# Linear attention and a highway layer: whole-row query packets, head-half exponentials, tanh + 1 on GpSimd

## The chip, the cores and the metric

The kernel runs on one core of one Trainium2 chip. The metric is the device time of one execution in microseconds; several runs are taken and the median counts.

## The reference

```
q_s = exp(q - max_d q);  q_s = q_s / (sum_d q_s + 1e-9)
k_s = exp(k - max_s k);  k_s = k_s / (sum_s k_s + 1e-9)
kv  = einsum('bhsd,bhse->bhde', k_s, v)
a   = einsum('bhsd,bhde->bhse', q_s, kv)          # 8 batches, 8 heads, 576 rows, 64 columns
x   = a.transpose(0, 2, 1, 3).reshape(4608, 512)
H   = maximum(x @ w_h, 0)
T   = 1 / (1 + exp(-(x @ w_t + b_t)))
out = T * H + (1 - T) * x                         # 4608 x 512, float32
```

q, k, v, the two 512 x 512 weights and the bias come as float32.

## The kernel before

**Tiles.** The 576 rows of a batch are 64 groups (partitions) of 9 neighbouring rows j = 0 to 8. A landing tile of k, q or v holds a batch as 128 partitions (two heads of a pair, 64 groups each) by 4 head pairs by 9 x 64 columns. The output is made in 36 tiles of 128 rows by 512 columns: four tiles for each batch (jp = 0 to 3, two values of j each) and one tile that two batches share, for the ninth row of each group. Nine tiles belong to a pair of batches: tiles 0 to 3 to batch 0, 4 to 7 to batch 1, tile 8 to both, and so on.

**Steps.** Everything is written as short steps whose order is the string `ORDER` (lines 15 to 61): a step is `name_tile_part` or `name_batch_part`, with a letter behind a colon where the engine is a choice (A is ScalarE, D is VectorE, P is GpSimd, called POOL in the profile). Each engine takes its instructions in that order, and so does SP, which issues nearly all transfers. Waits between engines follow from the data and from the reuse of buffers.

For a batch: `k`, `q`, `v` load (SP). `ek` takes the exponential of k (ScalarE, L252), `vc` casts v to 16 bits (L258, on any of three engines). `kv` is 72 small matmuls over j (L268). `kr` and `kn` take the reciprocal of the sums and scale into a block-diagonal tile `kvb` (VectorE, L280, L286). `eq` takes the exponential of q (ScalarE, L297, L303, L305), `qt` turns it with 18 transposes (TensorE, L316, L321) in three groups: j 0 to 3, j 4 to 7, j 8. `qc` copies the turned block out of PSUM (L330).

For a tile: `xu` multiplies turned q by `kvb` (L350), and the sums come as further columns. `rs` and `x` divide on VectorE (L359, L365). `xt` turns x (L372) and `xe` copies it out (L379). `bw` puts the bias into the bank `tps` (a ScalarE copy L387, or a matmul L389), `mt` adds x @ w_t to it (L399), `mh` makes x @ (w_h - 1)/2 in `gps` (L407). `th` is tanh of half the gate (ScalarE, L421, L423), `dd` is d = max(-x/2, gps) (VectorE, L427). The output is x + (tanh + 1) d. For 19 tiles `uu` does (tanh + 1) d in one VectorE instruction from PSUM (L442) and `oo` adds x on POOL (L460). For the 17 others, called lifted, which `ORDER` marks with `uu_i_0:P`, ScalarE writes tanh to SBUF and POOL does three two-input operations: `ee` e = d + x (L433), `uu` u = tanh d (L440), `oo` u + e (L460). `st` stores (L468, L476, L480).

**Buffers.** Landing tiles of each of k, q, v: 3. Tiles of x: 6. d, tanh, u, e: 3 each. Turned q: 4. Banks in PSUM: `tps` 2, `gps` 2, one area for `xu` and `kv`, one bank for `qt`, one for `xt`.

**Packets.** For batches 0 to 3 a query row is one run of 9 x 64 floats, 2304 bytes (batches 0 and 1 in two cuts). For batches 4 to 7 (`WIDE`) the query comes in a layout of its own: the main part in runs of four rows (1024 bytes), in two transfers, each on every second partition, and the row j = 4 of each group, 256 bytes, in a third transfer with an own place in `ORDER` (`q_4_9` to `q_7_9`). In the WIDE layout two output tiles that are mates are stored in one transfer of 128 partitions; for batches 0 to 3 in two transfers of 64 partitions each (`st_1_0`, `st_1_1`), in both cases in runs of 4096 bytes.

The copy of the turned queries, before:

```
t = eqp.tile([P, a, 4, s * NP], FP16, ...)
copy(t.rearrange("p a n t -> p (a n t)"), T[f"qps{b}_{g}"].rearrange("p a n s t -> p (a n s t)"))
```

Of the kernel before, what the change touches and what calls it, by code (L numbers as in the profile page):

```python
# [20 lines left out]
xe_1_0:D k_1_0 bw_1 xu_3_0 q_1_4 wtc_0 xu_0_1 rs_3_0 x_3_0 mh_1_0 wtc_2 xt_3_0 xe_3_0 xu_2_0 mt_1_0 rs_0_1 x_0_1 xt_0_0  # L21
eq_1_0 q_2_0 mt_3_0 th_1_0 rs_2_0 xe_0_0:D vc_1_3 ek_1_3 x_2_0 xt_0_1 th_3_0 qt_1_0 xe_0_1:D ek_1_2 dd_1 vc_1_0:A mh_0_0
xt_2_0 k_2_0 xe_2_0:D vc_1_2:D uu_1_0:P mh_0_1 bw_2 dd_0 qc_1_0:A mh_2_0 ee_1 dd_2 vc_1_1 v_2_0 kv_1_1 mh_3_0 ek_1_0
bw_0 kr_1_1 kn_1_1 dd_3 ek_1_1 mt_2_0 xu_5_1 rs_5_1 xu_4_1 kv_1_0 rs_4_1 k_3_0 x_5_1 th_2_0 kr_1_0 bw_5 oo_1_0 xt_5_1
mt_0_1 kn_1_0 mt_0_0 xu_5_0 x_4_1 rs_5_0 eq_1_1 ee_2 xu_4_0 qt_1_1 xe_5_1 mt_5_1 x_5_0 eq_1_2 qc_1_1 xt_5_0 xe_5_0:D
mh_5_1 th_0_0 q_3_0 rs_4_0 eq_2_2 uu_0_0 xu_6_0 rs_6_0 xt_4_1 qt_1_2 mt_5_0 mh_5_0 v_3_0 bw_4 x_4_0 x_6_0 xe_4_1 th_5_0
xt_4_0 mh_4_1 uu_3_0:P qc_1_2:A xe_4_0 xu_8_0 mh_4_0 mt_4_1 xt_6_0 ee_3 mt_4_0 eq_2_0 dd_5 oo_0_0 uu_2_0:P rs_8_0 oo_3_0
vc_2_2 uu_5_0 qt_2_0 x_8_0 ek_2_2 xe_6_0:D ek_2_0 k_4_0 dd_4 xu_7_0 rs_7_0 bw_6 th_4_0 oo_5_0 xt_8_0 mh_6_0 mt_6_0 q_4_9
x_7_0 xe_8_0:D xt_7_0 vc_2_0:A qc_2_0 eq_2_1 uu_4_0 oo_4_0 dd_6 bw_7:A kv_2_0 th_6_0 bw_8:A ek_3_0 ek_3_2 oo_2_0
xe_7_0:D mh_8_0 kr_2_0 kn_2_0 dd_8 mt_7_0 xu_9_0 rs_9_0 x_9_0 qt_2_1 th_7_0 mt_8_0 ee_6 q_4_0 qc_2_1 uu_6_0:P xu_10_0  # L30
oo_6_0 xt_9_0 rs_10_0 x_10_0 th_8_0 xe_9_0 mh_7_0 uu_8_0 qt_2_2 dd_7 bw_9 xu_12_0 eq_3_1 eq_3_0 xt_10_0 mt_9_0 mh_9_0
rs_12_0 x_12_0 xe_10_0:D uu_7_0:P xu_11_0 qc_2_2 xt_12_0 rs_11_0 qt_3_0 x_11_0 bw_10:A vc_3_2 dd_9 xe_12_0:D vc_3_0:A
th_9_0 uu_9_0 mh_10_0 oo_8_0 kv_3_0 kr_3_0 dd_10 ee_7 xt_11_0 mt_10_0 eq_3_2 qc_3_0:A bw_12:A oo_7_0 kn_3_0 mh_12_0
xu_14_0 ek_4_2 mt_12_0 xe_11_0:D v_4_0 v_5_0 qt_3_1 ek_4_0 rs_14_0 x_14_0 dd_12 xt_14_0 xe_14_0:D k_5_0 xu_13_0 th_10_0
bw_11:A rs_13_0 mh_11_0 mt_11_0 x_13_0 th_12_0 q_5_0 xt_13_0 qc_3_1:A oo_9_0 ee_10 dd_11 uu_10_0:P xu_15_0 qt_3_2
uu_12_0 rs_15_0 mh_14_0 eq_4_0 xe_13_0:D eq_4_1 mh_13_0 x_15_0 oo_10_0 xu_16_0 xt_15_0 qc_3_2 dd_14 rs_16_0 qt_4_0 ee_11
th_11_0 bw_14:A k_6_0 mt_14_0 x_16_0 qc_4_0 vc_4_2:A xe_15_0:D st_1_1 xu_17_0 st_1_0 rs_17_0 oo_12_0 x_17_0 qt_4_1 dd_13
bw_13:A mt_13_0 th_14_0 fill_0 vc_4_0 kv_4_0 uu_11_0:P eq_4_2 xt_16_0 qc_4_1:A mh_15_0 v_6_0 qt_4_2 vc_5_2 q_5_9 uu_14_0
xe_16_0:D st_3_1 oo_11_0 kr_4_0 th_13_0 oo_14_0 kn_4_0 bw_16:A bw_15:A xt_17_0 ek_5_0 xe_17_0:D dd_15 mh_16_0 xu_18_0
qc_4_2:A rs_18_0 mt_16_0 ek_5_2 x_18_0 vc_5_0 th_16_0 uu_13_0:P mt_15_0 dd_16 uu_16_0 xt_18_0 kv_5_0 kr_5_0 ee_13 ee_15  # L40
eq_5_0 xe_18_0:D kn_5_0 mh_17_0 mh_18_0 dd_17 xu_20_0 th_15_0 eq_5_1 bw_17:A rs_20_0 st_5_1 st_3_0 bw_18:A ek_6_0 qt_5_1
x_20_0 qc_5_1 mt_17_0 xu_21_0 rs_21_0 oo_13_0 xt_20_0 uu_15_0:P x_21_0 mt_18_0 ek_6_2 qt_5_0 xe_20_0:D oo_16_0 st_5_0
xu_19_0 xt_21_0 mh_20_0 oo_15_0 th_17_0 ee_17 dd_18 q_6_0 q_7_0 rs_19_0 th_18_0 st_7_1 uu_18_0 bw_20:A vc_6_0 qc_5_0:A
mt_20_0 x_19_0 xu_22_0 uu_17_0:P xe_21_0:D dd_20 rs_22_0 st_7_0 bw_21:A xt_19_0 mh_21_0 th_20_0 x_22_0 vc_6_2:A mt_21_0
kv_6_0 k_7_0 xe_19_0 st_10_0 uu_20_0 mh_19_0 th_21_0 oo_17_0 kr_6_0 xt_22_0 kn_6_0 dd_21 bw_19:A mt_19_0 xe_22_0:D
xu_23_0 v_7_0 bw_22 rs_23_0 mt_22_0 th_19_0 x_23_0 eq_5_2 bw_23:A qt_5_2 oo_18_0 xu_24_0 dd_19 xt_23_0 rs_24_0 mh_22_0
xe_23_0:D x_24_0 mh_23_0 eq_6_0 eq_6_1 qc_5_2 xt_24_0 xu_25_0 oo_20_0 dd_22 ee_21 rs_25_0 x_25_0 qt_6_0 xe_24_0:D
th_22_0 mt_23_0 uu_21_0:P ee_19 xu_26_0 qc_6_0 xt_25_0 st_10_1 bw_24:A st_12_1 oo_21_0 rs_26_0 eq_7_1 x_26_0 dd_23
eq_7_0 th_23_0 uu_22_0:P xe_25_0:D mh_24_0 fill_0 qt_7_0 mt_24_0 uu_19_0:P ee_22 xu_27_0 uu_23_0 rs_27_0 qc_7_0:A
oo_19_0 dd_24 xt_26_0 bw_25:A qt_6_1 oo_22_0 mh_25_0 xe_26_0 q_7_9 qc_6_1 x_27_0 mt_25_0 th_24_0 ek_7_2 xu_29_0 rs_29_0  # L50
mh_26_0 x_29_0 bw_27:A xt_27_0 uu_24_0:P qt_7_1 xe_27_0:D q_6_9 dd_25 xu_28_0 rs_28_0 xt_29_0 th_25_0 mt_27_0 mh_27_0
uu_25_0 oo_23_0 ek_7_0 vc_7_0 vc_7_2:A x_28_0 bw_26:A ee_24 kv_7_0 xe_29_0:D st_12_0:A dd_26 xt_28_0 th_27_0 kr_7_0
mt_26_0 kn_7_0 dd_27 bw_29:A eq_6_2 oo_25_0 oo_24_0 th_26_0 xe_28_0:D eq_7_2 mh_29_0 qc_7_1:A xu_31_0 mt_29_0 uu_26_0
ee_27 st_14_0 th_29_0 bw_28:A rs_31_0 x_31_0 mh_28_0 st_21_0 dd_29 xu_30_0 rs_30_0 x_30_0 xt_31_0 xe_31_0 dd_28 mt_28_0
th_28_0 qt_6_2 xu_33_0 oo_26_0 xt_30_0 st_14_1 qc_6_2:A mh_31_0 xe_30_0:D rs_33_0 st_17_0 bw_30:A x_33_0 mh_30_0 uu_28_0
xu_32_0 mt_30_0 uu_27_0:P uu_29_0:P xt_33_0 bw_31:A fill_0 rs_32_0 th_30_0 oo_27_0 st_16_1 ee_29 st_26_0 xe_33_0 qt_7_2
mt_31_0 dd_31 x_32_0 st_25_0 dd_30 xu_34_0 rs_34_0 oo_28_0 bw_33:A mh_33_0 xt_32_0 th_31_0 uu_31_0 oo_29_0 x_34_0
xe_32_0 qc_7_2:A mt_33_0 th_33_0 dd_33 mh_32_0 st_8_0 xu_35_0 bw_32:A xt_34_0 uu_33_0 ee_30 xe_34_0 bw_34:A rs_35_0
# [7 lines left out]
def kernel(  # L66
# [119 lines left out]
    WIDE = (4, 5, 6, 7)  # L186
    MAIN = 4 * 2 * 4 * D

    def flat_q(b):
        return landing("q", b).rearrange("p c f -> p (c f)")  # L190

    def load_q(e, b, j):
        if b in WIDE:
            head = S * D
            if j == 0:
                rows = q[b].rearrange("h (m t) d -> m h (t d)", m=NP)
                for u in range(2):
                    nc.sync.dma_start(flat_q(b)[u:P:2, 0:MAIN].rearrange("p (h f) -> p h f", h=H),
                                      rows[:, :, 5 * u * D:(5 * u + 4) * D])
            else:  # L200
                src = bass.AP(q.tensor, q.offset + b * H * head + 4 * D, [[NJ * D, P], [2 * head, 4], [1, D]])
                nc.sync.dma_start(flat_q(b)[:, MAIN:].rearrange("p (c d) -> p c d", c=4), src)
            return
# [89 lines left out]
    def eq(e, b, g):  # L293
        t = once(f"qe{b}", lambda: qep.tile([P, NJ, 4, D], FP16, tag="qe", name=f"qe_{b}"))
        j0, j1 = GROUPS[g]
        if b not in WIDE:
            nc.scalar.activation(t[:, j0:j1].rearrange("p j c d -> p c j d"),  # L297
                                 T[f"q32{b}"].rearrange("p c (j d) -> p c j d", j=NJ)[:, :, j0:j1], AF.Exp)
        elif g < 2:
            src = flat_q(b)[:, 0:MAIN].rearrange("p (c hh j d) -> p c hh j d", c=4, hh=2, j=4)  # L300
            dst = t.rearrange("p j c d -> p (j c d)")[:, 0:MAIN]
            dst = dst.rearrange("p (j hh c d) -> p c hh j d", j=4, hh=2, c=4)
            nc.scalar.activation(dst[:, :, g], src[:, :, g], AF.Exp)  # L303
        else:
            nc.scalar.activation(t[:, 8], flat_q(b)[:, MAIN:].rearrange("p (c d) -> p c d", c=4), AF.Exp)  # L305

    def qt(e, b, g):
# [3 lines left out]
        if b in WIDE and g < 2:  # L311
            main = T[f"qe{b}"].rearrange("p j c d -> p (j c d)")[:, 0:MAIN]
            main = main.rearrange("p (j hh kk f) -> p j hh kk f", j=4, hh=2, kk=2)
            for jp in (2 * g, 2 * g + 1):
                for n in range(4):
                    nc.tensor.matmul(t[:, jp % 2, n].rearrange("p s t -> p (s t)"), main[:, jp, n % 2, n // 2], idh,  # L316
                                     is_transpose=True, start=True, stop=True, skip_group_check=True)
            return
# [7 lines left out]
    def qc(e, b, g):  # L326
        copy = nc.scalar.copy if e == "A" else nc.vector.tensor_copy
        a, s = (2, 2) if g < 2 else (1, 1)
        t = eqp.tile([P, a, 4, s * NP], FP16, tag="eq" if g < 2 else "eq8", name=f"eq_{b}_{g}")
        copy(t.rearrange("p a n t -> p (a n t)"), T[f"qps{b}_{g}"].rearrange("p a n s t -> p (a n s t)"))  # L330
# [192 lines left out]
```

## Time and profile before

| | |
|---|---|
| median of 3 runs | 120.71 us (120.7 to 121.42) |
| profiled execution: span from first to last instruction | 119.0 us |
| its own time outside the span | not given apart; the median is 1.7 us above the span |
| TensorE matmul busy | 113.6 us, 1440 matmuls |
| VectorE busy | 94.6 us |
| ScalarE busy | 95.2 us |
| POOL busy | 91.2 us |
| moved | 40.08 MB, mean 337 GB/s |
| granted TensorE clock | 1.000 |

Busy time is the sum over an engine's instructions. Neighbouring rows overlap a little, since an instruction's pipeline drains while the next begins. Matmuls are pipelined, and their rows are longer than the time to the next one. The timeline gives start and duration; a group gives its count, its busy time and the mean of one; a wait is put down to what ended last before the instruction started.

### The profile page before, as it was taken

The page shows a single profiled execution, that of the slowest core. Times are in us where ns is not written, and L with a number is a line of the kernel's source. Part 1 is how long each engine was busy: PE and PEld are TensorE (multiplying, and loading weights), DVE is VectorE, ACT ScalarE, POOL GpSimd, SP SyncE. Part 2 cuts the span into 40 slices and gives each one's busy share as a digit, 9 for nine tenths or more (in the row PEclk, how much of TensorE's full clock was granted, in tenths as well). Part 3 has the DMA queues.
Part 4 walks back from the last instruction along what each step waited for, and adds up shares of the span by engine and source line. Part 5 has one row for each costly group of instructions (what it writes and reads, how often), then busy time and mean ns, then how long its engine had stood idle before and what let it go on. Part 6 is the DMA issues. An engine that isn't in the chain of part 4 may idle for free.

```text
span 119.0 us, 3609 instructions
## 1 busy us (share of the span) xinstructions
PE 113.6 (95%) x1440; PEld 71.3 (60%) x1440; DVE 94.6 (80%) x225; ACT 95.2 (80%) x144; POOL 91.2 (77%) x93
## 2 busy tenths in 40 slices
PE   5999999998999999999999999999999999999970
...
DVE  5604287696999988999999899879896999869880
ACT  4283779959699999999999999949979987578420
POOL 5002330099793998999999999999999979999960
...
DMA  2999999999999999999999999999999941995464
GB/s 67 374 395 373 388 376 380 393 371 387 395 383 392 392 388 382 334 378 386 387 370 370 401 387 392 355 365 392 398 377 343 299 109 61 388 292 234 176 271 169
DMA packets 22597, 40.08 MB, mean 337 GB/s; under 512 B 3251, under 2 KB 9651, under 8 KB 22581
## 3 DMA queue, kind: packets, MB, share of 16 engines
...
## 4 chain that ended last, share of the span: by engine, by line
PE 61%; DMA 17%; DVE 6%; ACT 6%; SPq 4%; issue 2%; DVEq 0%
PE tps L399 20%; PE gps L407 20%; DMA v<-in_v_dram 10%; DMA q<-in_q_dram 7%; PE turned L372 6%; PE xu L350 6%; PE kv L268 3%; SPq L183 3%; PE qps L316 3%; DVE u L442 2%; ACT ek L252 2%; PE qps L321 2%; DVE d L427 2%; ACT tps L387 1%; ACT th L421 1%
## 5 line engine op out<-in xcount | busy, mean ns | idle before, releaser
L399 PE MATMUL tps<-w16t,xT 128*128 128x512 f16 (+1 forms) x148 | 37.1, 373 | 0.0
L407 PE MATMUL gps<-w16h,xT 128*128 128x512 f16 x144 | 36.9, 379 | 0.0
L365 DVE TENSOR_TENSOR x<-xu,rs 128x512 f16<-128x512 f32 (+1 forms) x39 | 25.0, 645 | 1.7
L258 POOL CAST v<-v 128x1152 f16<-128x1152 f32 (+1 forms) x11 | 10.7, 976 | 19.3 <-DMA v<-in_v_dram 11.8
L427 DVE SCALAR_TENSOR_TENSOR d<-x,gps 128x512 f16<-128x512 f16 x36 | 24.2, 675 | 0.5 <-POOL e L433 0.3
L460 POOL TENSOR_TENSOR o<-u,x 128x512 f32<-128x512 f16 (+1 forms) x19 | 21.4, 1135 | 1.2 <-DVE u L442 1.2
L252 ACT ACTIVATE ek<-k 128x1152 f16<-128x1152 f32 (+1 forms) x20 | 18.9, 969 | 2.1 <-DMA k<-in_k_dram 2.0
L433 POOL TENSOR_TENSOR e<-d,x 128x512 f16<-128x512 f16 x17 | 19.7, 1164 | 0.7 <-DVE d L427 0.7
L440 POOL TENSOR_TENSOR u<-th,d 128x512 f16<-128x512 f16 x17 | 19.7, 1165 | 0.5 <-DVE rs L359 0.3
L460 POOL TENSOR_TENSOR o<-u,e 128x512 f32<-128x512 f16 x17 | 19.7, 1162 | 0.3
L399 PEld LDWEIGHTS <-xT 128*128 128x128 f16 x148 | 13.4, 98 | 10.3
L407 PEld LDWEIGHTS <-xT 128*128 128x128 f16 x144 | 12.6, 98 | 11.5 <-DVE xT L379 0.7
L167 PE MATMUL turned<-blank 128*128 128x256 f16 x111 | 16.1, 309 | 1.3 <-POOL blank L149 1.3
L387 ACT COPY tps<-ball 128x512 f32<-128x512 f32 x26 | 15.3, 593 | 1.6 <-DVE u L442 1.2
L167 PEld LDWEIGHTS <-blank 128*128 128x128 f16 x111 | 12.1, 111 | 4.3 <-POOL blank L149 1.3
L372 PE MATMUL turned<-idh,x 128*128 128x128 f16 x144 | 14.5, 219 | 0.1
L350 PE MATMUL xu<-kvb,eq 128*128 128x130 f16 (+1 forms) x160 | 14.5, 224 | 0.0
L350 PEld LDWEIGHTS <-eq 128*128 128x128 f16 (+1 forms) x160 | 10.3, 100 | 6.9 <-DVE x L365 2.2
L442 DVE SCALAR_TENSOR_TENSOR u<-tps,d 128x512 f16<-128x512 f32 (+1 forms) x20 | 13.1, 657 | 1.7 <-ACT tps L423 1.3
L423 ACT ACTIVATE tps<-tps 128x512 f32<-128x512 f32 (+1 forms) x20 | 11.2, 562 | 3.5 <-PE tps L399 3.3
L372 PEld LDWEIGHTS <-x 128*128 128x128 f16 x144 | 10.3, 98 | 4.8 <-DVE x L365 0.6
L379 DVE COPY xT<-turned 128x512 f16<-128x512 f16 (+1 forms) x28 | 11.3, 402 | 2.2 <-PE turned L372 1.7
...
## 6 DMA issues: line engine op xcount, KB each, us to landing
...
```

Of the source, the lines that this page charges most:

```text
L167: nc.tensor.matmul(spare, blank[:, 0:P], blank[:, 0:2 * P], start=True, stop=True, skip_group_check=True)
L252: nc.scalar.activation(t[:, :, c:c + n].rearrange("p j c d -> p c j d"), T[f"k32{b}"][:, c:c + n].rearrange("p c (j d) -> p c j d", j=NJ), ...
L350: nc.tensor.matmul(dst, turned_q(b, jp, n), kvb[b % NKV][:, hh, kk], start=True, stop=True, skip_group_check=True)
L365: nc.vector.tensor_mul(t[:, k0:k1], sums(i, k)[:, :, :, 0:64], T[f"rs{i}_{k}"][:, 0:k1 - k0].unsqueeze(3).to_broadcast([P, k1 - k0, 4, D]))
L372: nc.tensor.matmul(t[:, n], T[f"x{i}"][:, n * P:(n + 1) * P], idh, is_transpose=True, start=True, stop=True, skip_group_check=True)
L387: nc.scalar.copy(t[:, cs], ball[:, cs])
L399: nc.tensor.matmul(T[gate(i, k)][:, cs], T[f"xT{i}"][:, n], w16["t"][:, n, cs], start=False, stop=(n == parts[-1] and not first), skip_gro ...
L407: nc.tensor.matmul(t, T[f"xT{i}"][:, n], w16["h"][:, n], start=(first and n == parts[0]), stop=(n == parts[-1] and not (first and len(part ...
L427: nc.vector.scalar_tensor_tensor(t, T[f"x{i}"], -0.5, T[f"gps{i}"], op0=ALU.mult, op1=ALU.max)
L433: eng.tensor_add(T[f"e{i}"], T[f"d{i}"], T[f"x{i}"])
L440: eng.tensor_mul(t, T[f"th{i}"], T[f"d{i}"])
L460: eng.tensor_add(t[:, cs], T[f"u{i}"][:, cs], T[f"{'e' if lifted(i) else 'x'}{i}"][:, cs])
```

## The change

Queries of batches 4 to 7 are loaded as those of batches 2 and 3: one transfer a batch, 2304 bytes a packet. The WIDE layout goes, with its four separate transfers for j = 4. From batch 2 on the exponential of q is two instructions, one for each half of the heads and all nine rows, where it was three by rows; the third is gone, and `eq_2_1` stands ahead of `qt_2_0`, where it stood behind `qc_2_0`. `qc` writes the turned block so that the two values of j of a tile alternate from partition row to partition row: the two j of a group are neighbours in the tile, and two mates are stored by one transfer of 128 partitions in every batch (`st_1_1` to `st_16_1` are gone). For the lifted tiles `ee` is gone; `uu` is now two POOL instructions, g = (tanh + 1) * 1 and u = g d, and `oo` adds x. The rest of the order is as before.

```
     def load_q(e, b, j):
-        if b in WIDE:
-            ...
         js = slice(j * D, (NJ if j else Q_CUTS.get(b, NJ)) * D)
         nc.sync.dma_start(landing("q", b)[:, :, js], rows_of("q", b)[:, :, js])
@@ eq
-        if b not in WIDE: ...
-        elif g < 2: ...
-        else: ...
+        js, cs = (slice(*GROUPS[g]), slice(0, 4)) if b < 2 else (slice(0, NJ), slice(2 * g, 2 * g + 2))
+        nc.scalar.activation(t[:, js, cs].rearrange("p j c d -> p c j d"),
+                             T[f"q32{b}"].rearrange("p c (j d) -> p c j d", j=NJ)[:, cs, js], AF.Exp)
@@ qc
-        t = eqp.tile([P, a, 4, s * NP], FP16, ...)
-        copy(t.rearrange("p a n t -> p (a n t)"), T[f"qps{b}_{g}"].rearrange("p a n s t -> p (a n s t)"))
+        t = eqp.tile([P, a * 4, NP, s], FP16, ...)
+        copy(t.rearrange("p n t s -> p n s t"), T[f"qps{b}_{g}"].rearrange("p a n s t -> p (a n) s t"))
+        T[f"eq{b}_{g}"] = t.rearrange("p (a n) t s -> p a n (t s)", a=a)
@@ uu, lifted
-            eng.tensor_mul(t, T[f"th{i}"], T[f"d{i}"])
+            g = dp.tile([P, DM], FP16, tag="g16", name=f"g16_{i}")
+            nc.gpsimd.tensor_scalar(g, T[f"th{i}"], 1.0, 1.0, op0=ALU.add, op1=ALU.mult)
+            nc.gpsimd.tensor_mul(t, g, T[f"d{i}"])
@@ oo
-        eng.tensor_add(t[:, cs], T[f"u{i}"][:, cs], T[f"{'e' if lifted(i) else 'x'}{i}"][:, cs])
+        eng.tensor_add(t[:, cs], T[f"u{i}"][:, cs], T[f"x{i}"][:, cs])
@@ st
-        if b in WIDE: ... else: ...
+        j = 4 * (jp // 2) + (0 if both else jp % 2)
+        dst = bass.AP(out.tensor, out.offset + (b * S + j) * DM, [[NJ * DM, NP], [2 * DM, 2], [1, n]])
+        eng.dma_start(dst, o)
@@ ORDER
-  ee_1 ... ee_30 (17), eq_2_2 ... eq_7_2 (6), q_4_9 ... q_7_9 (4), st_1_1 ... st_16_1 (8)
-  qc_2_0 eq_2_1
+  eq_2_1 qt_2_0
```

More of the change, by code (lines that the diff above doesn't have):

```diff
@@ L20 @@
 whd_3 eq_0_2 xu_1_0 v_1_2 qc_0_1:A whc_2:A rs_0_0 rs_1_0 qt_0_2 x_1_0 x_0_0 qc_0_2:A fill_12 xt_1_0 whc_0:A v_1_0
[L21 to L58, printed above, removed]
+xe_1_0:D k_1_0 bw_1 xu_3_0 q_1_4 wtc_0 xu_0_1 rs_3_0 x_3_0 mh_1_0 wtc_2 xt_3_0 xe_3_0 xu_2_0 mt_1_0 rs_0_1 x_0_1
@@ new lines @@
+xt_0_0 eq_1_0 q_2_0 mt_3_0 th_1_0 rs_2_0 xe_0_0:D vc_1_3 ek_1_3 x_2_0 xt_0_1 th_3_0 qt_1_0 xe_0_1:D ek_1_2 dd_1
+vc_1_0:A mh_0_0 xt_2_0 k_2_0 xe_2_0:D vc_1_2:D uu_1_0:P mh_0_1 bw_2 dd_0 qc_1_0:A mh_2_0 dd_2 vc_1_1 v_2_0 kv_1_1
+mh_3_0 ek_1_0 bw_0 kr_1_1 kn_1_1 dd_3 ek_1_1 mt_2_0 xu_5_1 rs_5_1 xu_4_1 kv_1_0 rs_4_1 k_3_0 x_5_1 th_2_0 kr_1_0 bw_5
+oo_1_0 xt_5_1 mt_0_1 kn_1_0 mt_0_0 xu_5_0 x_4_1 rs_5_0 eq_1_1 xu_4_0 qt_1_1 xe_5_1 mt_5_1 x_5_0 eq_1_2 qc_1_1 xt_5_0
+xe_5_0:D mh_5_1 th_0_0 q_3_0 rs_4_0 uu_0_0 xu_6_0 rs_6_0 xt_4_1 qt_1_2 mt_5_0 mh_5_0 v_3_0 bw_4 x_4_0 x_6_0 xe_4_1
@@ new lines @@
+th_5_0 xt_4_0 mh_4_1 uu_3_0:P qc_1_2:A xe_4_0 xu_8_0 mh_4_0 mt_4_1 xt_6_0 mt_4_0 eq_2_0 dd_5 oo_0_0 uu_2_0:P rs_8_0
+oo_3_0 vc_2_2 uu_5_0 eq_2_1 qt_2_0 x_8_0 ek_2_2 xe_6_0:D ek_2_0 k_4_0 dd_4 xu_7_0 rs_7_0 bw_6 th_4_0 oo_5_0 xt_8_0
+mh_6_0 mt_6_0 x_7_0 xe_8_0:D xt_7_0 vc_2_0:A qc_2_0 uu_4_0 oo_4_0 dd_6 bw_7:A kv_2_0 th_6_0 bw_8:A ek_3_0 ek_3_2
+oo_2_0 xe_7_0:D mh_8_0 kr_2_0 kn_2_0 dd_8 mt_7_0 xu_9_0 rs_9_0 x_9_0 qt_2_1 th_7_0 mt_8_0 q_4_0 qc_2_1 uu_6_0:P
+xu_10_0 oo_6_0 xt_9_0 rs_10_0 x_10_0 th_8_0 xe_9_0 mh_7_0 uu_8_0 qt_2_2 dd_7 bw_9 xu_12_0 eq_3_1 eq_3_0 xt_10_0 mt_9_0
@@ new lines @@
+mh_9_0 rs_12_0 x_12_0 xe_10_0:D uu_7_0:P xu_11_0 qc_2_2 xt_12_0 rs_11_0 qt_3_0 x_11_0 bw_10:A vc_3_2 dd_9 xe_12_0:D
+vc_3_0:A th_9_0 uu_9_0 mh_10_0 oo_8_0 kv_3_0 kr_3_0 dd_10 xt_11_0 mt_10_0 qc_3_0:A bw_12:A oo_7_0 kn_3_0 mh_12_0
+xu_14_0 ek_4_2 mt_12_0 xe_11_0:D v_4_0 v_5_0 qt_3_1 ek_4_0 rs_14_0 x_14_0 dd_12 xt_14_0 xe_14_0:D k_5_0 xu_13_0
+th_10_0 bw_11:A rs_13_0 mh_11_0 mt_11_0 x_13_0 th_12_0 q_5_0 xt_13_0 qc_3_1:A oo_9_0 dd_11 uu_10_0:P xu_15_0 qt_3_2
+uu_12_0 rs_15_0 mh_14_0 eq_4_0 xe_13_0:D eq_4_1 mh_13_0 x_15_0 oo_10_0 xu_16_0 xt_15_0 qc_3_2 dd_14 rs_16_0 qt_4_0
@@ new lines @@
+th_11_0 bw_14:A k_6_0 mt_14_0 x_16_0 qc_4_0 vc_4_2:A xe_15_0:D xu_17_0 st_1_0 rs_17_0 oo_12_0 x_17_0 qt_4_1 dd_13
+bw_13:A mt_13_0 th_14_0 fill_0 vc_4_0 kv_4_0 uu_11_0:P xt_16_0 qc_4_1:A mh_15_0 v_6_0 qt_4_2 vc_5_2 uu_14_0 xe_16_0:D
+oo_11_0 kr_4_0 th_13_0 oo_14_0 kn_4_0 bw_16:A bw_15:A xt_17_0 ek_5_0 xe_17_0:D dd_15 mh_16_0 xu_18_0 qc_4_2:A rs_18_0
+mt_16_0 ek_5_2 x_18_0 vc_5_0 th_16_0 uu_13_0:P mt_15_0 dd_16 uu_16_0 xt_18_0 kv_5_0 kr_5_0 eq_5_0 xe_18_0:D kn_5_0
+mh_17_0 mh_18_0 dd_17 xu_20_0 th_15_0 eq_5_1 bw_17:A rs_20_0 st_3_0 bw_18:A ek_6_0 qt_5_1 x_20_0 qc_5_1 mt_17_0
@@ new lines @@
+xu_21_0 rs_21_0 oo_13_0 xt_20_0 uu_15_0:P x_21_0 mt_18_0 ek_6_2 qt_5_0 xe_20_0:D oo_16_0 st_5_0 xu_19_0 xt_21_0
+mh_20_0 oo_15_0 th_17_0 dd_18 q_6_0 q_7_0 rs_19_0 th_18_0 uu_18_0 bw_20:A vc_6_0 qc_5_0:A mt_20_0 x_19_0 xu_22_0
+uu_17_0:P xe_21_0:D dd_20 rs_22_0 st_7_0 bw_21:A xt_19_0 mh_21_0 th_20_0 x_22_0 vc_6_2:A mt_21_0 kv_6_0 k_7_0 xe_19_0
+st_10_0 uu_20_0 mh_19_0 th_21_0 oo_17_0 kr_6_0 xt_22_0 kn_6_0 dd_21 bw_19:A mt_19_0 xe_22_0:D xu_23_0 v_7_0 bw_22
+rs_23_0 mt_22_0 th_19_0 x_23_0 bw_23:A qt_5_2 oo_18_0 xu_24_0 dd_19 xt_23_0 rs_24_0 mh_22_0 xe_23_0:D x_24_0 mh_23_0
@@ new lines @@
+eq_6_0 eq_6_1 qc_5_2 xt_24_0 xu_25_0 oo_20_0 dd_22 rs_25_0 x_25_0 qt_6_0 xe_24_0:D th_22_0 mt_23_0 uu_21_0:P xu_26_0
+qc_6_0 xt_25_0 bw_24:A oo_21_0 rs_26_0 eq_7_1 x_26_0 dd_23 eq_7_0 th_23_0 uu_22_0:P xe_25_0:D mh_24_0 fill_0 qt_7_0
+mt_24_0 uu_19_0:P xu_27_0 uu_23_0 rs_27_0 qc_7_0:A oo_19_0 dd_24 xt_26_0 bw_25:A qt_6_1 oo_22_0 mh_25_0 xe_26_0 qc_6_1
+x_27_0 mt_25_0 th_24_0 ek_7_2 xu_29_0 rs_29_0 mh_26_0 x_29_0 bw_27:A xt_27_0 uu_24_0:P qt_7_1 xe_27_0:D dd_25 xu_28_0
+rs_28_0 xt_29_0 th_25_0 mt_27_0 mh_27_0 uu_25_0 oo_23_0 ek_7_0 vc_7_0 vc_7_2:A x_28_0 bw_26:A kv_7_0 xe_29_0:D
@@ new lines @@
+st_12_0:A dd_26 xt_28_0 th_27_0 kr_7_0 mt_26_0 kn_7_0 dd_27 bw_29:A oo_25_0 oo_24_0 th_26_0 xe_28_0:D mh_29_0 qc_7_1:A
+xu_31_0 mt_29_0 uu_26_0 st_14_0 th_29_0 bw_28:A rs_31_0 x_31_0 mh_28_0 st_21_0 dd_29 xu_30_0 rs_30_0 x_30_0 xt_31_0
+xe_31_0 dd_28 mt_28_0 th_28_0 qt_6_2 xu_33_0 oo_26_0 xt_30_0 qc_6_2:A mh_31_0 xe_30_0:D rs_33_0 st_17_0 bw_30:A x_33_0
+mh_30_0 uu_28_0 xu_32_0 mt_30_0 uu_27_0:P uu_29_0:P xt_33_0 bw_31:A fill_0 rs_32_0 th_30_0 oo_27_0 st_26_0 xe_33_0
+qt_7_2 mt_31_0 dd_31 x_32_0 st_25_0 dd_30 xu_34_0 rs_34_0 oo_28_0 bw_33:A mh_33_0 xt_32_0 th_31_0 uu_31_0 oo_29_0
@@ L59 @@
+x_34_0 xe_32_0 qc_7_2:A mt_33_0 th_33_0 dd_33 mh_32_0 st_8_0 xu_35_0 bw_32:A xt_34_0 uu_33_0 xe_34_0 bw_34:A rs_35_0
 uu_30_0:P mt_32_0 st_23_0 st_16_0 st_19_0 mh_34_0 x_35_0 xt_35_0 mt_34_0 th_32_0 st_28_0 dd_32 bw_35_1 oo_31_0 oo_33_0
@@ L184, in load_kv @@
         return step
[L186 to L190, printed above, removed]
     def load_q(e, b, j):
-        if b in WIDE:
[L194 to L203, printed above, removed]
         js = slice(j * D, (NJ if j else Q_CUTS.get(b, NJ)) * D)
@@ L294, in eq @@
         t = once(f"qe{b}", lambda: qep.tile([P, NJ, 4, D], FP16, tag="qe", name=f"qe_{b}"))
[L295 to L305, printed above, removed]
+        js, cs = (slice(*GROUPS[g]), slice(0, 4)) if b < 2 else (slice(0, NJ), slice(2 * g, 2 * g + 2))
+        nc.scalar.activation(t[:, js, cs].rearrange("p j c d -> p c j d"),
+                             T[f"q32{b}"].rearrange("p c (j d) -> p c j d", j=NJ)[:, cs, js], AF.Exp)
     def qt(e, b, g):
```

30 lines of the change are left out of this document (4 added, 26 removed).

## The prediction

> **What bounds the kernel now.** I read the page from the top: busy time, the slices, the chain that ended last, then the groups by form, and last the order of time on single engines.
>
> ```profile
> PE 113.6 (95%) x1440; PEld 71.3 (60%) x1440; DVE 94.6 (80%) x225; ACT 95.2 (80%) x144; POOL 91.2 (77%) x93
> ...
> PE   5999999998999999999999999999999999999970
> ...
> DVE  5604287696999988999999899879896999869880
> ACT  4283779959699999999999999949979987578420
> POOL 5002330099793998999999999999999979999960
> ...
> DMA  2999999999999999999999999999999941995464
> ```
>
> All four engines and the DMA stand at 8 and 9 tenths from slice 10 to slice 30 (a slice is 3 us). So the busy share names no bound, and the chain has to.
>
> ```profile
> PE 61%; DMA 17%; DVE 6%; ACT 6%; SPq 4%; issue 2%; DVEq 0%
> ```
>
> In its order of time the chain is DMA until the v of batch 1 has landed (25.7 us) and from 45 to 112 us nothing but matmuls, each group of four 512-column ones in 0.86 us, that is 215 ns each with no gap. TensorE sets the end. A change that takes no matmul away can gain only what TensorE waits, and loses whatever it makes TensorE wait. In the list of waits from 30 to 112 us nothing on TensorE waits for a DMA or for POOL; it waits 2.2 us for `x`, about 1 us for `xT`, 0.5 us for `eq`. How near each step is to being late can be read by setting the end of its producer against its own start: `xt` starts 0.3 to 0.7 us after its `x` ends in most tiles, `mh` 0.1 to 1 us after its `xe`. About 0.06 us is the least that ever stands there.
>
> **The change part by part.** The groups by form that price it (mean ns of one behind the busy time):
>
> ```profile
> L365 DVE TENSOR_TENSOR x<-xu,rs 128x512 f16<-128x512 f32 x33 | 22.7, 688 | 1.6
> L433 POOL TENSOR_TENSOR e<-d,x 128x512 f16<-128x512 f16 x17 | 19.7, 1164 | 0.7 <-DVE d L427 0.7
> L440 POOL TENSOR_TENSOR u<-th,d 128x512 f16<-128x512 f16 x17 | 19.7, 1165 | 0.5 <-DVE rs L359 0.3 <-ACT th L421 0.2
> L252 ACT ACTIVATE ek<-k 128x1152 f16<-128x1152 f32 x12 | 13.5, 1164 | 0.0
> L379 DVE COPY xT<-turned 128x512 f16<-128x512 f16 x25 | 10.4, 416 | 1.3 <-PE turned L372 0.9 <-ACT tps L423 0.2
> L297 ACT ACTIVATE qe<-q 128x1024 f16<-128x1024 f32 x8 | 8.4, 1059 | 2.0 <-DMA q<-in_q_dram 2.0
> L258 POOL CAST v<-v 128x1152 f16<-128x1152 f32 x7 | 8.1, 1153 | 1.8 <-DMA v<-in_v_dram 1.8
> L330 DVE COPY eq<-qps 128x1024 f16<-128x1024 f16 x8 | 5.5, 682 | 0.0
> L258 POOL CAST v<-v 128x576 f16<-128x576 f32 x4 | 2.7, 667 | 17.5 <-DMA v<-in_v_dram 10.0 <-DVE xT L379 7.5
> L365 DVE TENSOR_TENSOR x<-xu,rs 128x256 f16<-128x256 f32 x6 | 2.4, 408 | 0.1
> L305 ACT ACTIVATE qe<-q 128x256 f16<-128x256 f32 x4 | 1.7, 414 | 0.0
> ```
>
> *Matmuls.* None goes: a batch keeps its 18 transposes in `qt` (219 ns each on both lines), and `xu` reads the same 128 columns. Zero.
>
> *Queries in 2304-byte packets.* In the packet records of the trace a 1024-byte packet takes 50 ns, a 256-byte one 18, a 2304-byte one 100. A late batch costs 1024 x 50 + 512 x 18 = 60 us of one DMA engine, 3.8 us over sixteen; then 512 x 100 = 51 us, 3.2 us. Four batches save 2.4 us of DMA, and SP makes eight issues less. The late tails (issued at 61.8, 82.3 and 83.6 us) go; the whole query comes in the place of its main part, 0.36 us more bytes and 0.6 us less packets, so it lands no later, and today its exponential starts 1.3 us (batch 5) to 4 us after the last main packet. Cover: TensorE. As no load is waited for after 38 us, I count nothing; if loads set the pace it would be all of the 2.4 (a rival below).
>
> *Merged stores.* Eight SP issues of about 0.5 us go, the same bytes in the same 4096-byte pieces. The stores wait for POOL, nobody waits for them but the end, and the last stores (tiles 32 to 35) are unchanged. Zero.
>
> *Query exponentials by head halves.* From batch 2 on, two of 1152 elements (1164 as `ek`) replace 1059 + 1059 + 414. Successive ScalarE rows overlap by 0.11, so a batch goes from 2.2 to 2.1 us: six batches, 0.6 us less ScalarE time, spread; counted as nothing. But every transpose now needs both halves, so `eq_2_1` is moved forward past `ek_2_2`, `ek_2_0`, `th_4` and `vc_2_0`. In order of time ScalarE has, before:
>
> ```profile
> 34.08 1.08 ACT L297 ACTIVATE qe<-q 128x1024 f16<-128x1024 f32 x1
> 35.04 2.23 ACT L252 ACTIVATE ek<-k 128x1152 f16<-128x1152 f32 x2
> 37.14 0.61 ACT L423 ACTIVATE tps<-tps 128x512 f32<-128x512 f32 x1
> 37.88 1.15 ACT L258 CAST v<-v 128x1152 f16<-128x1152 f32 x1
> 38.94 1.05 ACT L297 ACTIVATE qe<-q 128x1024 f16<-128x1024 f32 x1
> ```
>
> The fourth row is `vc_2_0`; TensorE's `kv_2` starts at 39.13, just behind it. With both halves first: 34.08 + 1.06 + 1.06 = 36.20, the two `ek` to 38.31, `th_4` to 38.8, `vc_2_0` to 39.94. `kv_2` at 40.0: 0.87 us late. TensorE has its queue in order, so `mh_8`, `mt_7` and `xu_9` stand behind it, and `kr_2`, `kn_2`, `x_9` on VectorE behind those. `qt_2_0` waits about 0.4 us too, ahead of `kv_2` and inside the same delay. The early `eq_2_2` that goes (0.4 us at 31.9) gives nothing back: ScalarE waits for TensorE after it.
>
> *`qc` writes every second element.* Of the 17 copies of 1024, eight are on VectorE. Two-byte rows with both sides dense: 682 for 1024, 416 for 512, so 0.52 ns per element. Rows with a four-byte side: 688 for 512, 408 for 256, 1.09 per element. The new target has neighbours of the stream four bytes apart, so I put it with the second kind: 688 + 512 x 1.09 = 1.25 us, 0.57 more than 0.68. The lower bound is no growth, if only the type of the element counts; a gain is excluded, as no element goes. ScalarE's copies (1.01 us, already at its one-at-a-time rate: 1.06 for the same number of four-byte ones) stay.
>
> The Trainium skill, "VectorE: DVE Perf Modes", section "What auto-detection actually checks", says that two results per cycle need every tensor to be 16-bit with a step of one. No row here shows a spaced two-byte target. By that rule the copy grows as I took it; without it the sum would end at the lower bound, 121.6.
>
> Where the 0.57 lands, copy by copy. `qc_1_1` (31.14 to 31.82) releases `xu_6` at 31.91 directly:
>
> ```profile
> 31.14 0.69 DVE L330 COPY eq<-qps 128x1024 f16<-128x1024 f16 x1
> ```
>
> ```profile
> PEld L350 <- DVE eq L330: 0.3, 1, 0.3
> ```
>
> The first line is from the order of time, the second from the waits of the weight loads, on which `xu` begins. TensorE is already waiting there, so 0.55 is lost; the ScalarE chain above starts behind TensorE and moves with it, so this adds to the 0.87. `qc_0_0` lies before 14 us, where TensorE runs filler: nothing. `qc_2_0` lies inside the delay of `kv_2`. `qc_2_1` is followed by `x_10`, whose `xt` has 0.70 us, and then VectorE idles 0.24: covered. `qc_4_0`: `xe_16` has 0.57 behind an idle of 0.27: covered. `qc_5_1`: `xt_19` has 0.47, `xe_21` 0.36 and VectorE has no idle between: 0.25 lost. `qc_6_0` and `qc_6_1` come 3.8 us apart with VectorE full, so `xu_29`, 0.83 us behind `qc_6_1`, sees 1.14: 0.3 lost. Together 1.1. Without these covers it would be 7 x 0.57 = 4.0.
>
> *tanh + 1 on GpSimd instead of d + x.* Of 17 tiles each loses a two-input add (1.16, as the multiplication that stays) and gets a one-input operation. No such row; nearest is the one-input cast, 667 and 1153 for 576 and 1152 elements, which makes 0.61 for 512. Bounds: 0.61 and, with its two arithmetic steps counted as a two-input operation, 1.16. I take 0.61: POOL sheds 17 x 0.55 = 9.4 us. Gain on the path: none, as TensorE and, but for 0.3 us, VectorE do not wait for POOL's `e`, and the last `o` waits for VectorE's `u`. Cost: tanh + 1 must follow `th`, where d + x could run ahead, and `x` is now held until `oo`. Today's margin between `oo` of a lifted tile and the `x` six later is 0.6 to 4 us, except `oo_2` to `x_9`, -0.2, and that `x` comes over 1 us later anyway. Zero.
>
> Sum: 0.55 + 0.87 + 0.25 + 0.3 = 1.97. Span 119.0 + 1.97 = 121.0. The profiled execution's own time is given only as its span; the median of the runs, 120.71, is 1.7 longer, and I keep that: **122.7**.
>
> **The rivals.**
>
> *Half of it is not there (0.27).* The spaced copy keeps 0.68. Then only `kv_2` is late: 119.0 + 0.87 + 1.7 = 121.6; if later waits of TensorE, some 0.5 to 1 us in ten, swallow part, 121. For it: no row shows a spaced store. Against: only dense rows have the short time.
>
> *VectorE becomes the bound (0.13).* From 30 to 60 us it is busy 9.1 to 9.5 of every 10 us, and xu, x, xt, xe form a loop through it. If each copy's growth shows whole: 4.0 + 0.87, so 125.6. Against: idle stretches of 0.24 to 0.93 us stand behind four of the seven.
>
> *The loads set the pace, and the change is faster (0.07).* The DMA row has nines to slice 31. If TensorE's work is only stretched to the rate of the loads, then saving 2.4 us of packets moves the last k and v, `kv_7` and all behind it forward by that: 118.3. It decides only from the point where a load is waited for. For it: 1.05 of DMA share from 10 to 95 us. Against: the only late wait for a load is POOL's 1.8 us at 37.9; `kv_7` has its casts 0.6 us and more ahead of it.
>
> *The GpSimd operation is dear (0.05).* POOL idles 4 us between 30 and 110, so from 1.16 + 4/17 = 1.4 us on it sets the pace. At twice the add, 2.33, it adds 19.8 us less those 4: 136. Against: one input, as the cast.
>
> **How the numbers follow.** Forecast 0.48. Its own range is 121.3 to 124. The two larger slow cases bring the top to 125.2 (the 136 is left out), the half case brings the bottom to 120.8. About 1% (1.2 us) is what a measurement of this kernel can tell. Slower by more: the forecast (less 0.02 that falls inside), VectorE and POOL: 0.64. Within: 0.02 + 0.27 - 0.01 = 0.28. Faster: the loads, and that 0.01 of the half case together with POOL relief: 0.08.
>
> **What would show it.** `eq<-qps` 128x1024 on VectorE near 1.25 us (0.68: the half case). `kv` of batch 2 starting near 40.5 instead of 39.13 with a ScalarE cast just before it. A group on POOL with `g` near 0.6 us, POOL's busy time near 82 us, and idle in its late slices. The busy DMA slices ending sooner, with TensorE's last matmul about 2 us later all the same. The forecast is wrong if TensorE's last matmuls end before 114 us, if `kv_2` is not late, or if new waits of `x` for `o` or of the load queue for ScalarE take the first places of the wait list.

## The result and the profile after

The changed kernel takes 124.54 us (median of 4 runs, 124.23 to 124.78) against 120.99 us for the kernel before beside it: ratio 1.029, 95% interval 1.026 to 1.033. It is slower by 3.6 us, where 2.0 us were forecast, and above the forecast's own range of 121.3 to 124. The profiled execution spans 123.0 us (its time 124.78) against 119.0.

Busy times and slices of the page after, as shown for before:

```profile
PE 115.0 (94%) x1440; PEld 71.1 (58%) x1440; DVE 98.8 (80%) x225; ACT 97.0 (79%) x138; POOL 83.2 (68%) x93
...
DMA  3999999999999999999999999999950040995464
```

VectorE has 4.2 us more work, ScalarE 1.8 us more though six instructions are gone, POOL 8 us less. The DMA row leaves its nines three slices earlier, at slice 29 instead of 32 (the last packet of a 2304-byte load ends at 88.7 us instead of 90.3, and the 256-byte tails, which ended at 92.5, are gone). TensorE still ends 4 us later: the loads do not set the pace.

The chain that ended last, by engine and by line:

```profile
PE 49%; DVE 20%; DMA 17%; ACT 5%; SPq 3%; issue 2%; DVEq 0%; ACTq 0%
PE gps L373 17%; PE tps L365 15%; DMA v<-in_v_dram 10%; DVE eq L296 7%; DMA q<-in_q_dram 7%; PE xu L316 6%; DVE x L331 5%; PE turned L338 5%; PE kv L250 3%; SPq L182 3%; PE qps L287 3%; DVE d L393 2%; DVE u L403 2%; DVE rs L325 1%; ACT eq L296 1%
```

VectorE has gone from 6% to 20% of it. The copies of the turned queries (L296, `qc`) on VectorE are 7%, all seven that come after 14 us; before, a single one of them stood in the chain, with 0.68 us (0.6%). The groups by form of the parts that changed (mean ns of one behind the busy time):

```profile
L278 ACT ACTIVATE qe<-q 128x1152 f16<-128x1152 f32 x12 | 13.4, 1162 | 0.0
L296 ACT COPY eq<-qps 128x1024 f16<-128x1024 f16 x8 | 10.5, 1317 | 1.0 <-PE qps L287 1.0
L400 POOL TENSOR_SCALAR g<-th 128x512 f16<-128x512 f16 x17 | 10.5, 617 | 4.5 <-ACT th L387 4.1 <-DVE xT L345 0.4
L296 DVE COPY eq<-qps 128x1024 f16<-128x1024 f16 x8 | 10.4, 1305 | 0.0
L296 ACT COPY eq<-qps 128x256 f16<-128x256 f16 x5 | 1.8, 367 | 0.0
L296 DVE COPY eq<-qps 128x256 f16<-128x256 f16 x3 | 0.8, 281 | 0.0
```

A copy of 1024 takes 1305 ns on VectorE (682 before) and 1317 on ScalarE (1012 before). The row of ScalarE's copies before:

```profile
L330 ACT COPY eq<-qps 128x1024 f16<-128x1024 f16 x8 | 8.1, 1012 | 1.0 <-PE qps L316 0.6 <-PE qps L321 0.5
```

The copies of 256 have one j, so their target stays dense; they stay at 281 and 367. The gate's first step takes 617 ns.

**Where TensorE falls behind.** For each step of TensorE I set its start after the change against its start before; the difference only moves at some dozen places, and these add up to the whole 4.0 us:

| step | late by | what it waits for | spare time it had before |
|---|---|---|---|
| kv_1_0 | 0.46 | `ek` behind the longer `qc_1_0` on ScalarE (and 0.2 from a load of v that landed later in this execution) | 0.05 |
| xu_6 | 0.58 | `qc_1_1`, its data | 0.08 |
| qt_2_0, kv_2 | 0.35 + 0.53 | `eq_2_1`, then `vc_2_0` behind it | |
| xu_12 | 0.41, of which 0.26 comes back at xt_10 | `x_10`, which frees the area of `xu` | 0.21 |
| xu_15, mt_14 | 0.20 | `qc_3_1` on ScalarE, the data of xu_15 (0.14), then other work of ScalarE | 0.14 |
| qt_4_1 | 0.44 | `qc_4_0`, which frees the one bank of `qt` | 0.26 |
| xu_19, xt_21 | 0.33 | `x_21`, which frees the area of `xu` | 0.40 |
| xu_22 | 0.14 | `x_19`, the same | 0.24 |
| xt_26 | 0.22 | `xe_25`, which frees the bank of `xt` | 0.43 |
| xu_29 | 0.63 | `x_27`, which frees the area of `xu` | 0.24 |

Two of them in the order of time of TensorE, first `qt_4_1`, then `xu_29` (start, duration, what; in brackets the idle time before and its releaser):

```profile
61.97 0.42 PE L316 MATMUL xu<-kvb,eq 128*64 128x130 f16 x8
62.77 0.61 PE L287 MATMUL qps<-idh,qe 128*128 128x128 f16 x8 [0.38 <-DVE eq L296]
...
93.19 1.03 PE L365 MATMUL tps<-w16t,xT 128*128 128x512 f16 x4
94.68 0.41 PE L316 MATMUL xu<-kvb,eq 128*128 128x130 f16 x4 [0.47 <-DVE x L331]
```

and VectorE's side of the second:

```profile
91.49 0.68 DVE L403 SCALAR_TENSOR_TENSOR u<-tps,d 128x512 f16<-128x512 f32 x1
92.08 0.20 DVE L325 RECIPROCAL rs<-xu 128x8 f32<-128x8 f32 x1
92.20 0.63 DVE L393 SCALAR_TENSOR_TENSOR d<-x,gps 128x512 f16<-128x512 f16 x1
92.75 1.30 DVE L296 COPY eq<-qps 128x1024 f16<-128x1024 f16 x1
93.95 0.68 DVE L331 TENSOR_TENSOR x<-xu,rs 128x512 f16<-128x512 f32 x1
```

`xu_29` does not wait for the copy as its data but for `x_27` behind the copy: until x is read, the area of `xu` is taken. TensorE starts 0.05 us after that x ends. Before, the same x and the same step stood about 0.24 us apart:

```profile
89.72 0.68 DVE L365 TENSOR_TENSOR x<-xu,rs 128x512 f16<-128x512 f32 x1
90.64 0.40 PE L350 MATMUL xu<-kvb,eq 128*128 128x130 f16 x4
```

In the waits of the weight loads `x` has grown from 2.2 to 4.3 us, and the copies from 0.5 (ScalarE) and 0.3 (VectorE):

```profile
PEld L316 <- DVE x L331: 4.3, 11, 1.0
...
PEld L316 <- ACT eq L296: 1.4, 3, 0.8
...
PEld L316 <- DVE eq L296: 0.9, 1, 0.9
```

### The profile page after: what moved, and what is told of

It reads as the page before. It is cut to its first block, busy times and chain, and to the rows that moved or that the text cites. A ratio compares the mean times of both kernels' runs of the same rounds, so it can differ in the third digit from the quotient of the medians.

```text
span 123.0 us, 3587 instructions
## 1 busy us (share of the span) xinstructions
PE 115.0 (94%) x1440; PEld 71.1 (58%) x1440; DVE 98.8 (80%) x225; ACT 97.0 (79%) x138; POOL 83.2 (68%) x93
## 4 chain that ended last, share of the span: by engine, by line
PE 49%; DVE 20%; DMA 17%; ACT 5%; SPq 3%; issue 2%; DVEq 0%; ACTq 0%
PE gps L373 17%; PE tps L365 15%; DMA v<-in_v_dram 10%; DVE eq L296 7%; DMA q<-in_q_dram 7%; PE xu L316 6%; DVE x L331 5%; PE turned L338 5%; PE kv L250 3%; SPq L182 3%; PE qps L287 3%; DVE d L393 2%; DVE u L403 2%; DVE rs L325 1%; ACT eq L296 1%
## 5 line engine op out<-in xcount | busy, mean ns | idle before, releaser
L421 POOL TENSOR_TENSOR o<-u,x 128x512 f32<-128x512 f16 (+1 forms) x36 | 40.6, 1142 | 8.5 <-DVE u L403 8.0
L401 POOL TENSOR_TENSOR u<-g,d 128x512 f16<-128x512 f16 x17 | 19.6, 1155 | 3.3 <-DVE rs L325 1.1
L278 ACT ACTIVATE qe<-q 128x1152 f16<-128x1152 f32 (+2 forms) x18 | 18.5, 1056 | 2.2 <-DMA q<-in_q_dram 2.2
L400 POOL TENSOR_SCALAR g<-th 128x512 f16<-128x512 f16 x17 | 10.5, 617 | 4.5 <-ACT th L387 4.1
L296 ACT COPY eq<-qps 128x1024 f16<-128x1024 f16 (+1 forms) x13 | 12.4, 952 | 1.0 <-PE qps L287 1.0
```

The lines of the kernel that those rows point to most:

```text
L278: nc.scalar.activation(t[:, js, cs].rearrange("p j c d -> p c j d"), T[f"q32{b}"].rearrange("p c (j d) -> p c j d", j=NJ)[:, cs, js], AF.Exp)
L296: copy(t.rearrange("p n t s -> p n s t"), T[f"qps{b}_{g}"].rearrange("p a n s t -> p (a n) s t"))
L401: nc.gpsimd.tensor_mul(t, g, T[f"d{i}"])
L421: eng.tensor_add(t[:, cs], T[f"u{i}"][:, cs], T[f"x{i}"][:, cs])
```

## The experiments

Theory A after the result: the spaced copies, on both engines, cost most of the loss, the moved exponential 0.88 us, and the gate on POOL, the packets and the stores nothing. Rivals: the gate and the longer life of x are part of it (P); only VectorE's copies matter (V). Some of the kernels below leave the rows of the result in other places than they belong; they are there for their time alone.

**The spaced copies alone, in the kernel before** (`spaced_before`):

```
-        t = eqp.tile([P, a, 4, s * NP], FP16, ...)
-        copy(t.rearrange("p a n t -> p (a n t)"), T[...].rearrange("p a n s t -> p (a n s t)"))
+        t = eqp.tile([P, a * 4, NP, s], FP16, ...)
+        copy(t.rearrange("p n t s -> p n s t"), T[...].rearrange("p a n s t -> p (a n) s t"))
```

> The kernel before with the spaced copies alone; nothing else is changed, so the 128 rows of most tiles come out in another order. Theory A: 3.1 us of loss, span 122.1, time about 124.0. Rival J (the spaced copies hurt only together with the later kv_2 and the loads of the changed kernel): under 122.5.

Measured: 123.83 against 120.78, ratio 1.024 (1.021 to 1.027). This one edit brings 3.05 us, and TensorE's late steps are mostly those of the table, without the 0.35 at qt_2_0 and the 0.53 at kv_2. J falls.

**Dense copies, with the store's pattern turned to match** (`dense_all`; `dense_dve` and `dense_act` do it for the copies of one engine only):

```
-        dst = bass.AP(..., [[NJ * DM, NP], [2 * DM, 2], [1, n]])
+        dst = bass.AP(..., [[2 * DM, 2], [NJ * DM, NP], [1, n]])
```

> The changed kernel with the copies of the turned queries dense again (rows of a tile in the order of the two j, and the store's pattern turned to match). Theory A (the spaced copies on both engines cost 3.15 us of the 4.0, the moved exponential 0.88, the other parts nothing): copies back to 0.68 us on VectorE and 1.01 on ScalarE, span near 119.9, time about 121.9, 0.7% above before; kv of batch 2 still the one late step. Rival P (the three-step gate on POOL and x held until the last add are part of the loss): above 123, with waits of x for o. Rival D (the copies' growth is only the visible end of a shortage of VectorE): near 120.9, no loss.

> The changed kernel with VectorE's copies of the turned queries dense, ScalarE's still spaced. Theory A: 2.5 us of the loss go (0.58 at xu_6, 0.16 at xu_12, 0.43 at qt_4_1, 0.45 around xu_19, 0.89 around xu_29), 0.46 at kv_1, 0.88 at kv_2 and 0.2 later stay: span 120.6, time 122.4. Rival V (only VectorE's copies matter, the growth on ScalarE is hidden): the same as with all copies dense, within 0.2 us.

> The changed kernel with ScalarE's copies of the turned queries dense, VectorE's still spaced. Theory A: only the 0.46 at kv_1 and about 0.2 later go: span 122.3, time 124.0. Rival V (ScalarE's growth is hidden): no difference from the changed kernel, 124.5.

Measured: 246.11, 176.94 and 176.98 us. All three miss, and say nothing of the copies: the stores became the bound. The page of the first has

```profile
GB/s 230 383 379 386 384 388 391 390 391 392 389 172 55 54 230 217 112 160 219 53 53 55 54 126 57 55 88 53 52 52 53 53 52 52 52 51 72 52 70 39
```

Loads run at 390 GB/s, a store alone at 52. In the packet records two 4096-byte packets are in flight for 131 us of the time and hardly ever more, 159 ns each: 2 x 4096 / 159 = 51.5 GB/s. With the 64 groups outermost, in the changed kernel, 16 of them are in flight for 6.0 us, longer than any other number. The Trainium skill, "DMA: Bandwidth & Descriptors", section "Why a DMA increments its semaphore by 16 and not by 1", says that the number of engines follows from the slowest dimension of the two patterns, the largest number up to 16 that divides both; here that is 2. The trace agrees: two packets in flight. This is what the alternating rows are for: in the kernels here, one transfer brings two tiles to their places with more than two packets in flight only where the rows alternate, whether a load arranges that (batches 4 to 7 before) or the copy.

**Dense copies with two stores of 64 partitions for a pair**, as the kernel before has them for batches 0 to 3; batch 7 left as changed (`dense_all2`), and for the copies of VectorE alone (`dense_dve2`) and of ScalarE alone (`dense_act2`):

```
+        if T[f"dense{b}_{jp // 2}"]:
+            for u in range(2):
+                dst = bass.AP(out.tensor, out.offset + (b * S + j + 2 * u) * DM, [[NJ * DM, NP], [1, n]])
+                eng.dma_start(dst, o[64 * u:64 * u + 64])
+            return
```

> The changed kernel with dense copies for batches 0 to 6 and two stores of 64 partitions for each of their pairs, as before had them; batch 7 (two spaced copies on ScalarE, the stores of the end) stays as changed. Theory A: of the loss only the moved exponential of batch 2 stays, 0.88 us at kv_2: span 119.9, time 121.7. Rival P (gate on POOL, x held longer, or the packets of the queries are part of the loss): above 122.5.

> The changed kernel with dense copies where VectorE makes them (and two stores for those pairs), spaced where ScalarE does. Theory A: 0.46 at kv_1, 0.88 at kv_2 and 0.2 later stay: span 120.6, time 122.3. Rival V (ScalarE's growth is hidden): the same as with all copies dense, within 0.2 us.

> The changed kernel with dense copies where ScalarE makes them, batch 7 left out, spaced where VectorE does. Theory A: 0.46 at kv_1 and about 0.2 later go: span 122.3, time 123.9. Rival V: as the changed kernel, 124.5.

**The same with batch 2's exponentials by rows in their old places** (`dense_rows2`):

```
-        js, cs = (...) if b < 2 else (slice(0, NJ), slice(2 * g, 2 * g + 2))
+        js, cs = (...) if b < 3 else (slice(0, NJ), slice(2 * g, 2 * g + 2))
-  uu_5_0 eq_2_1 qt_2_0 ... qc_2_0 uu_4_0
+  rs_4_0 eq_2_2 uu_0_0 ... uu_5_0 qt_2_0 ... qc_2_0 eq_2_1 uu_4_0
```

> As the one before it, and batch 2's exponentials again in three by rows, in their old places. Theory A: nothing of the loss is left, 120.8, at best 0.5 below for the shorter packets' time and POOL's 8 us; kv_2 at 39.1 again. Rival P: 121.5 or more, the price of gate, packets and halves together.

Measured: 122.60, 122.70, 123.69 and 121.99 us, against 120.74. The first and the last lie 0.9 and 1.2 us above what theory A gives, and both within what was put down as rival P's sign; the two in the middle lie 0.4 above and 0.2 below theory A's, and the second, 0.1 from the first, is also what rival V gives. Yet TensorE's last steps are only 0.53 and 0.23 us late in the first and the last; the rest comes behind. POOL in the end phase of `dense_all2`:

```profile
108.99 4.49 POOL L427 TENSOR_TENSOR o<-u,x 128x512 f32<-128x512 f16 x4
114.92 1.95 POOL L427 TENSOR_TENSOR o<-u,x 128x512 f32<-128x512 f16 x2 [1.44 <-DMA out_dram<-o]
```

The last add waits for a store to free its buffer: SP has eight issues in a row there, from 102.5 to 110.7 us, where the kernel before has some of these pairs in one store. In `dense_rows2` that wait is 1.16 us. So the second stores have a price of their own, in the end phase; these kernels mix two things, and they can't decide between A, P and V.

**The copies alone, stores untouched.** The next kernels leave the store as in the changed kernel, so most rows land in other places. All dense (`dense_perm`), and with batch 2's exponentials as before (`perm_rows2`):

> The changed kernel with all copies of the turned queries dense and its stores as they are (one of 128 partitions for a pair), so that the rows of most tiles go to other places; it takes the copies alone away, with no second store in the end phase. Theory A: only the moved exponential of batch 2 stays (0.88 at kv_2, some 0.2 given back at xt_10): span 119.8, time 121.5. Rival P (gate, packets, halves are part of the loss): above 122.

> As the one before it, with batch 2's exponentials in three by rows in their old places; rows go to other places as there. Theory A: nothing of the loss is left: 120.8, within 0.3 of before. Rival P: 121.3 or more. Rival S (with dense copies the saved packets and POOL's 8 us show): 120.2 or less.

Measured: 121.16 against 120.88, ratio 1.002 (0.9997 to 1.005), and 120.66, ratio 0.998 (0.996 to 0.9996). With dense copies 3.4 of the 3.6 us are gone. Theory A had 121.5, and 120.9, which rival D of `dense_all` gave for dense copies, is as near; but D has no place for the 0.5 us that go with batch 2's exponentials as before. With them nothing is left, and the sum of gate, packets, halves from batch 3 on and merged stores is a gain of 0.2%, with an interval that ends just short of no difference. P falls, for the sum of these parts and for the gate alone (below); packets and merged stores were not run one by one. Both copies are back to their old times:

```profile
L296 ACT COPY eq<-qps 128x1024 f16<-128x1024 f16 x8 | 8.1, 1012 | 0.3 <-PE qps L287 0.3
L296 DVE COPY eq<-qps 128x1024 f16<-128x1024 f16 x8 | 5.5, 683 | 0.0
```

One engine's copies dense, the other's spaced (`perm_dve`: VectorE's dense; `perm_act`: ScalarE's dense):

```
-        t = eqp.tile([P, a * 4, NP, s], FP16, ...)
+        if e != "A":        # perm_act: e == "A"
+            t = eqp.tile([P, a, 4, s * NP], FP16, ...)
+            ...
+        else:
+            t = eqp.tile([P, a * 4, NP, s], FP16, ...)
```

> The changed kernel with VectorE's copies dense and ScalarE's spaced, stores as they are (rows of some tiles go to other places). Theory B (each spaced copy costs what TensorE waits for it: VectorE's 2.6 us, ScalarE's 0.9): 122.0, TensorE's end lag 1.2 us, a step of 0.5 at kv_1 and of 0.3 at xu_22. Rival V (ScalarE's growth is hidden, all 3.4 us are VectorE's): 121.2, as with all copies dense.

> The changed kernel with ScalarE's copies dense and VectorE's spaced, stores as they are (rows of some tiles go to other places). Theory B: 123.7, TensorE's end lag 2.9 to 3.1 us, the steps at xu_6, qt_4_1 and xu_29 unchanged. Rival V: 124.5, as changed.

Measured: 122.14 (ratio 1.010, 1.008 to 1.013) and 123.86 (1.026, 1.023 to 1.029). Over 121.16 with all dense, ScalarE's copies cost 1.0 us and VectorE's 2.7; V falls. Their sum, 3.7, is 0.3 more than both cost together, so a little of one hides behind the other. One place shows it: xu_22 is 0.31 us late with ScalarE's copies spaced alone (there it waits for `qc_5_0`, its data), 0.13 with VectorE's alone, and 0.14 in the changed kernel.

**The other parts alone, in the kernel before.** One step moved (`move_before`), and the gate (`gate_before`):

```
-  uu_5_0 qt_2_0 ... qc_2_0 eq_2_1 uu_4_0
+  uu_5_0 eq_2_1 qt_2_0 ... qc_2_0 uu_4_0
```

> The kernel before with one step moved: the second exponential of batch 2 ahead of the transposes, as in the changed kernel. Theory A: vc_2_0 and so kv_2 0.9 us late, 0.6 to 0.9 left at the end: 121.5. Rival E (TensorE waits for the load of v there anyway and takes the delay back later): 120.8.

```
-  ee_1 ... ee_30
-            eng.tensor_mul(t, T[f"th{i}"], T[f"d{i}"])
+            nc.gpsimd.tensor_scalar(g, T[f"th{i}"], 1.0, 1.0, op0=ALU.add, op1=ALU.mult)
+            nc.gpsimd.tensor_mul(t, g, T[f"d{i}"])
```

> The kernel before with the gate alone: no d + x, tanh + 1 as a one-input operation on GpSimd, x added last. Theory A: POOL sheds 8 to 9 us, and the time stays, 120.8 within 0.3. Rival P (tanh + 1 stands behind th, x is held until o): 121.3 or more. Rival S (POOL was a hidden bound): 120.3 or less.

Measured: 121.03, ratio 1.002 (1.0002 to 1.0038), and 120.90, ratio 1.001 (0.999 to 1.003). The move delays `kv_2` behind the cast of v, by 0.67 us where 0.87 had been worked out (in this kernel `qt_2_0` does not need the moved exponential):

```profile
38.59 0.39 PE L372 MATMUL turned<-idh,x 128*128 128x128 f16 x4
39.57 0.80 PE L268 MATMUL kv<-v,ek 64*64 64x65 f16 x72 [0.60 <-ACT v L258]
```

Of the 0.67, 0.26 us come back at `xt_10`, and in time 0.02 to 0.46 us stay (the medians are 0.15 apart): theory A's 121.5 is missed. Inside the change it is more: 0.5 us, from `dense_perm` to `perm_rows2`, which also puts batch 2's exponentials back from halves to rows. The gate sheds 8 us of POOL (83.0 busy) and changes nothing.

Of the kernels with every row in its place none was faster than the kernel before.

## Why the prediction was right or wrong, point by point

- **What bounds.** Right. TensorE sets the end, no matmul went, and every late microsecond is found as a wait of TensorE. The loads ended earlier (the 2304-byte ones by 1.6 us, all of them by 3.8) and the kernel became slower, so the rival of the loads is refuted. The slices were read too evenly: POOL has a 3 in slice 12 and VectorE a 6 in slice 30; nothing hangs on it.
- **The parts at nothing.** Gate, packets, merged stores: right, shown for the gate by `gate_before` and for their sum by `perm_rows2`; single prices of packets and stores, which could have opposite signs, are not shown. The gate's first step was put at 0.61 and measured 0.617.
- **The moved exponential.** Put at 0.87. At `kv_2` it measured 0.88 (0.35 ahead of it at `qt_2_0`, 0.53 at it), but only 0.15 to 0.5 us last to the end. This term was too high: the chain was right, and the give-back behind it, 0.26 us at `xt_10`, was left out. Its error is in the other direction than those of the next points: with this term right the forecast would have been further off, so part of its nearness is luck.
- **The copy on VectorE.** The step of 0.57 was nearly right (0.62): with the spaced target the copy loses its short time and costs a little more than the 1246 ns worked out from four-byte rows (1305; the dense 256 stay at 281). This agrees with the rule of the Trainium skill that the prediction cites ("VectorE: DVE Perf Modes", "What auto-detection actually checks"). There are 16 copies of 1024, eight on each engine, not 17; the sum does not use that number.
- **"ScalarE's copies stay."** Wrong, and the first term that failed: growth on ScalarE was put at nothing, since these copies were held to be at the one-at-a-time rate already. They went from 1012 to 1317 ns, 1.0 us of the loss by `perm_dve`. The first price of it is at `kv_1_0`, where `ek` stands behind `qc_1_0`. Why ScalarE pays is not shown; the 256-element copies, dense in both, do not. The target's step and its split into runs of 64 came together, and no run separates them.
- **"Where the 0.57 lands", 1.1 us.** The second term that failed, too small: 2.7 by `perm_act`. `xu_6` was right (0.55 put, 0.58 measured). The other covers were read from a producer to the consumer of its data: x to `xt`, `qc` to the `xu` that reads it. With one area or bank each for `xu`, `qt` and `xt`, the reader also holds back the next writer of that bank, and there the spare time was 0.2 to 0.4 us, where the prediction had read 0.36 to 0.83. `qc_2_1` and `qc_4_0`, called covered, cost 0.15 and 0.44; `qc_5_1` 0.3 to 0.5 instead of 0.25; `qc_6_0` and `qc_6_1` 0.85 instead of 0.3. The idle stretches of VectorE were counted as cover too; the longer of them are waits for `xu` or `kv` and move with TensorE.
- **The rivals.** "Half of it is not there" fell with the first line of the groups. "VectorE becomes the bound" was nearest in kind: VectorE is 20% of the chain. It is not the bound throughout: of seven times 0.62 only 2.7 us show, and what stays hidden is above all `qc_2_0` and `qc_2_1`, beside the late `kv_2`. This rival's own sum was 125.6, while the top of the range, said to come from it, is given as 125.2; how is not told.
